# Score tiles placed 64 bytes lower, 64 rows to each score product, and shorter product times in the clocks that order TensorE's work

## The chip, the cores and the metric

The kernel runs on one core of a Trainium2 chip. The metric is the device time of one execution in microseconds, the median of the runs. Engines are named as in the profile: PE is TensorE, DVE is VectorE, ACT is ScalarE, POOL is GpSimd, SP is SyncE (it issues most DMAs here).

## The reference

A layer norm feeds two branches, an attention of 32 heads with 18 columns each and a bilinear feed-forward block; the second, through a SiLU, gates the first.

```python
x = A_x                                   # 1 x 2048 x 576
xn = _layernorm(x, axis=-1)
# _A_ref: H = 32, Dh = 18
scores = jnp.einsum("bhqd,bhkd->bhqk", q, k) * (Dh ** -0.5)
p = _softmax(scores, axis=-1)
o = jnp.einsum("bhqk,bhkd->bhqd", p, v)   # then @ wo
# _B_ref: F = 4608
h = (xn @ w_gate) * (xn @ w_up)           # then h @ w_down
g = _silu(_B_ref(xn, ...))
return x + s * g                          # s: the attention's result
```

All is float32.

## The kernel before

Operands are split into a high and a low part in the fp32r type, and a product of two float32 numbers is made of three: high by high, low by high and high by low. In the scores the three stand below each other in one product: a stack of 3 x 18 = 54 rows, R in the code.

**First stage** (0 to about 193 us): the norm, the turned input (xc, xcx), and the columns of q, k and v. `qk_block(b, c)` makes one block of 128 columns of q and k for one chunk of 512 tokens with 14 products of 128 rows (L493). Its weights are in tiles named wgu, wq or ninth; those of blocks 4 and 5 are in a tile wq2 (wq in the profile) that lies in the pool `early`, at the right end of the memory, with the input and its norm. When the stage is nearly over, the pool `early` is closed and the pool `stk` takes its place with three tiles of 128 x 2048: `turning` and two called `whole`. GpSimd fills them with ones (L638, L641), and `load_stack` (L322) fetches a head's q and k into rows 0 to 53 and 64 to 117.

**The head loop** (about 193 to 2525 us) does the attention and the feed-forward block together. TensorE's array is split in two halves of 64 rows, and the two halves run different products at the same time, r = 0 and r = 1 in the code. The products are:

- `a_item` (L709): 128 queries by 512 keys, 54 rows, for the maximum of each row, which DVE takes (L711). Nearly all on half 0.
- `b_item` (L761): the same scores turned, with two more rows (R + 2 = 56) that hold the negated maximum against ones in the other tile; ACT takes the exponential (L763). Nearly all on half 1.
- `gu_op` (L813): 27 products of 64 rows by 512 columns for each 128 columns of gate (half 1) and of up (half 0).
- `down_op` (L874): products of 64 rows by 288 columns with the weights wd.
- `pv_group` (L772): the exponentials by the values, on all 128 rows with 32 columns. These come in visits, for which both halves are finished first.

Two score products are in `turning` and `whole` at once: one of the two tiles gives the fixed operand, the other the streamed one.

The order of the head loop is worked out when the program is built. `order()` keeps one clock for each half, `clk[0]` and `clk[1]`, and the times at which DVE, ACT and GpSimd come free, and writes down, for the half whose clock is behind, the next product: a score product when it is due and its bank is free by the clocks, otherwise one of the streams `glu` and `down`. Each product moves its half's clock on by a fixed length: 0.231 for a product of 512 columns, 0.132 for one of 288. From the same lengths come the sums `part` and `span`, and with them the pace at which the score products fall due (`pace`, `keep_course`). TensorE then carries out the products strictly in the order written down.

**Last stage** (from about 2525 us): the heads' result by wo (L1469), the gate and the sum.

Of the kernel before, what the change touches and what calls it, by code (L numbers as in the profile page):

```python
# [20 lines left out]
FT = mybir.dt.float32  # L21
# [20 lines left out]
def kernel(  # L42
# [10 lines left out]
    nc = tc.nc  # L53
    _, S, D = x.shape
    F = w_gate.shape[1]
    H = 32
    DH = D // H
    assert S == 2048 and D == 576 and F % 256 == 0
    NT = S // 128
# [40 lines left out]
    ep = early.enter_context(tc.tile_pool(name="early", bufs=1, side="right"))  # L100
# [66 lines left out]
    clk, free, split_at = [0.0, 0.0], {"DVE": 0.0, "ACT": 0.0, "POOL": 0.0}, {}  # L167
# [50 lines left out]
    units = [(c, q) for c in range(NCH) for q in range(NF2)]  # L218
# [90 lines left out]
    R = 3 * DH  # L309
# [257 lines left out]
    def w_now(i):  # L567
        wq[i], todo = w_split(raws[i], 1 if i == 4 else 2, ep if i == 2 else pp if i == 4 else None)
        for f, a in todo:
            f(*a)  # L570
# [36 lines left out]
    for c in range(NCH):  # L607
        if c + 2 < NCH:
            load_x(c + 2)
        for b in range(3):  # L610
            qk_block(b, c)
            if c == 0 and b == 0:
                w_now(2)
        if c + 1 < NCH:
            to_columns(c + 1)
        for b in range(3, 6):
            qk_block(b, c)
            if c == 1 and b == 3:
                v_split(c)
            if b < 5 and c + 2 < NCH:  # L620
                norm(c + 2, (0, 1) if b == 3 else (2, 3))
            if c in (1, 2):
                x_store(c, range(3 * (b - 3), 3 * (b - 2)))
            if c == 0 and b == 3:
                v_fetch(1)
            if c == NCH - 1 and b == 3:
                w_now(3)
        if c == 1:
            w_fetch(3)
            for t in range(4):  # L630
                v_block(t)
            w_fetch(4)
        if c == 2:
            w_now(4)
    early.close()
    stk = ctx.enter_context(tc.tile_pool(name="stk", bufs=1, side="right", reuse_waits="tile"))
    turning = stk.tile([128, S], FR, name="turning")
    nc.gpsimd.memset(turning.bitcast(FT), 1.0)  # L638
    whole = [stk.tile([128, S], FR, name=f"whole{i}") for i in range(2)]
    for w in whole:  # L640
        nc.gpsimd.memset(w.bitcast(FT), 1.0)  # L641
    vmore = ExitStack()
    more_rows(vmore.enter_context(tc.tile_pool(name="vmore", bufs=1, side="right")), 2)
    g_load(0)
# [23 lines left out]
    n = 8  # L668
# [22 lines left out]
    with ExitStack() as mid:  # L691
# [3 lines left out]
        def load_v(g):  # L695
            vt[g] = mp.tile([128, NT, 2 * (DH + 1)], FT, name="vt", bufs=2)
            nc.sync.dma_start(vt[g].rearrange("p t (h d) -> p t h d", h=2), sv[:, 2 * g:2 * g + 2, :].rearrange("(t p) h d -> p t h d", p=128))

        mx = {}

        def a_item(h, i, r=0, tag="a"):

            t, c = divmod(i, 4)
            if i == 0:
                mx[h] = mp.tile([128, NT, 4], FT, name="mx", bufs=1)
            q, k = stacks_of(h, r)
            p = bank(tag, 2)
            rows = slice(64 * r, 64 * r + R)
            nc.tensor.matmul(p, q[rows, t * 128:(t + 1) * 128], k[rows, c * 512:(c + 1) * 512],  # L709
                             start=True, stop=True)  # L710
            nc.vector.tensor_reduce(mx[h][:, t, c:c + 1], p, axis=AX.X, op=OP.max)  # L711
# [42 lines left out]
        def b_item(h, i, r=1, tag="b"):  # L754
            t, c = divmod(i, 4)
            if c % 2 == 0:
                pt[t, c // 2] = mp.tile([128, 2, 512], FT, name="pt", bufs=PT)
            q, k = stacks_of(h, r)
            p = bank(tag, 2)
            rows = slice(64 * r, 64 * r + R + 2)  # L760
            nc.tensor.matmul(p, k[rows, t * 128:(t + 1) * 128], q[rows, c * 512:(c + 1) * 512],  # L761
                             start=True, stop=True)
            nc.scalar.activation(pt[t, c // 2][:, c % 2, :], p, AF.Exp, scale=scale)  # L763
# [37 lines left out]

        hs, us = {}, {}
        TERMS = [t for b in range(9) for t in ((b, b, 0), (9 + b, b, 0), (b, b, 1))]
        half = [slice(0, 64), slice(64, 128)]

        def gu_start(r, n):
            ready(gdone, n)
# [213 lines left out]
            nc.sync.dma_start(wos[1].bitcast(FT), swo[:, 8:10, :])  # L1021

        passed, xdone, xhalf = {}, [], set()

        def stream(r, kind):

            def glu(n):
                c, q = units[n // 2]
                box = []
                for k in range(len(TERMS)):  # L1030
                    def work(k=k):
                        if k == 0:
                            box.append(gu_start(r, n))
                        gu_op(r, n, box[0], k)
                        if q == NF2 - 1 and n % 2 and k % 3 == 2 and c < NCH - 1:
                            b = k // 3
                            if (c, b) in xhalf:
                                x_block(c + 1, b)
                                there["x", c + 1, b] = moved(clk[r] + 0.5, 0.40)
                            xhalf.add((c, b))  # L1040
                        if n == 2 * len(units) - 1 and k == 13:
                            xdone.append(r)
                            if len(xdone) == 2:
                                wo_fetch()
                        if k == len(TERMS) - 1:
                            highs.append((gate_end if r else up_end)(n, box[0]))
                    end = (("DVE", 0.685) if r else ("ACT", 0.595)) if k == len(TERMS) - 1 else None
                    yield 0.231, k == 0, work, end, ("g", n, k), len(TERMS)

            def down(u, n):  # L1050
                own = alone(u, n)
                key = u, n, r * own
                s, i = divmod(n, 2)
                for k in range(len(DTERMS)):
                    def work(k=k):
                        if (own or r == 0) and k == 0:
                            passed[key] = down_start(r, u)
                        down_op(r, u, s, i, passed[key], k, {"POOL": nc.gpsimd, "ACT": nc.scalar, "DVE": nc.vector}[soonest()])
                        if (own or r) and k == len(DTERMS) - 1:
                            acts.append(by_act(u, i, clk[r] + 0.33))  # L1060
                            down_end(u, s, i, passed.pop(key), acts[-1])
                    end = None
                    if (own or r) and k == len(DTERMS) - 1:
                        end = (None, 0.0)
                    yield 0.132, (own or r == 0) and k == 0, work, end, ("d", u, 6 * n + k), len(DTERMS)

            if kind == "g":
                for n in range(2 * len(units)):
                    yield from glu(n)
            else:  # L1070
                for u in range(len(units)):
                    for n in range(8):
                        yield from down(u, n)
# [4 lines left out]
        N = 64  # L1078
        TOTAL = H * N
# [18 lines left out]
        due, jobs, rows_done = [], [], {}  # L1098
        there, queue = {}, [0.0]
        na = nb = 0  # L1100
        part_work = len(units) * (2 * 27 * 0.231 + 4 * 12 * 0.132)
        part = part_work + (TOTAL + N + LEAD) * 0.231
        span = part + H * NT * (0.858 + 0.06)
        QUICK, LAST = 0.65, 0.6
        pace = (PACE * span - QUICK * N - LAST * (N + LEAD)) / (TOTAL - N)
# [3 lines left out]
        def keep_course(now):  # L1109

            left = part_work - (gone[0] + gone[1]) / 2
            left += (2 * TOTAL - na - nb) * 0.1155 + (H * NT - nb // 4 + len(due)) * 0.918
            course[:] = [na, now, (EASE * left - TAIL - LAST * (N + LEAD)) / (TOTAL - na)]

        def a_goal(i):
# [24 lines left out]
        def a_next(r=0):  # L1140
            nonlocal na
            h, i = divmod(na, N)
            stack_turn(0, h, i, 1)
            tag = a_tag()
            a_item(h, i, r, tag)
            slot = turn[tag] % 2
            turn[tag] += 1
            banks[tag][slot] = engine("DVE", clk[r] + 0.43, 0.685) + SPARE
            clk[r] += 0.231
            na += 1  # L1150
            if na % 32 == 0 and N <= na < TOTAL - N:
                keep_course(clk[r])
            if i == N - 1:
                max_fold(h)
                max_split(h, engine("DVE", 0.0, 0.2))
# [5 lines left out]
        def b_next(r=1):  # L1161
            nonlocal nb
            h, i = divmod(nb, N)
            stack_turn(64, h, i, 0)
            if i == 16 and h % 2 == 0 and h // 2 + 1 < H // 2:
                load_v(h // 2 + 1)
            tag = b_tag()
            b_item(h, i, r, tag)
            slot = turn[tag] % 2
            turn[tag] += 1  # L1170
            end = engine("ACT", clk[r] + 0.43, 0.596)
            banks[tag][slot] = end + SPARE
            clk[r] += 0.231
            nb += 1
            if i % 4 == 3:
                due.append((h, i // 4, end + 0.1))
# [343 lines left out]
```

## Time and profile before

| | us |
|---|---|
| median of 3 runs | 2594.28 (2593.94 to 2596.97) |
| span of the profiled execution, first to last instruction | 2590.2 |
| head loop in it | about 193.5 to 2525 |
| products in the head loop | L813 7776, L709 and L761 4096 together, L874 6912 |
| visits of the value products | 67 |

The page gives of the profiled execution its span alone; what lies around it is in the runs' times. A row of groups reads: line, engine, operation, what is written and read, shapes, count, then the busy time, the mean duration of one and the idle time before it. A row of the timeline reads: start and length in us, engine, line, operation, tiles, shape, and the number of equal instructions merged in it. The profile counts a few records of score products under other bank names, so that L709 and L761 show fewer than 2048 each.

### The profile page before, as it was taken

To read this page: it belongs to the slowest core of one execution; us is meant where nothing else is said; L and a number is where in the kernel's file an instruction comes from. 1 tells how busy PE (TensorE), PEld (TensorE's weight loads), DVE (VectorE), ACT (ScalarE), POOL (GpSimd) and SP (SyncE) were. 2 spreads that over 40 slices of the span, in tenths; PEclk is the share of its full clock that TensorE was granted. 3 is DMA by queue.
4 is the path that set the end of the run, shared out by engine and by line. 5 is a ranking of instruction groups with operands and counts; after the bars stand their busy time and mean duration, and the time that the engine had idled before them with its cause. 6 is when DMAs were issued, how large, how long until landed. Compare 5 with 4: busy or idle time off the path is not lost.

```text
span 2590.2 us, 59629 instructions
## 1 busy us (share of the span) xinstructions
PE 2582.3 (100%) x24439; PEld 2124.4 (82%) x24439; DVE 1815.2 (70%) x2996; ACT 1551.5 (60%) x3092; POOL 677.0 (26%) x701
## 2 busy tenths in 40 slices
PE   9999999999999999999999999999999999999999
PEld 8899877888888888888877877778888877877889
DVE  7209777776777778777777877777777777777238
ACT  4224677766766666666666666666666666666621
POOL 3114444434431222222111222111111222221016
PEclk9999999999999999999999999999999999999999
DMA  7899767677653444444454443444444444443357
GB/s 237 258 301 260 200 184 196 184 189 214 178 189 111 141 164 136 150 162 160 143 166 148 142 142 126 137 146 159 121 158 124 145 150 142 133 139 112 125 202 253
DMA packets 186641, 435.65 MB, mean 168 GB/s; under 512 B 51104, under 2 KB 112192, under 8 KB 156160
## 3 DMA queue, kind: packets, MB, share of 16 engines
q1 hardware_dynamic: 184208, 423.88, 53.0%
q0 software_dynamic: 2160, 7.96, 0.8%
q8 instruction: 192, 3.15, 0.5%
q14 instruction: 81, 0.66, 0.1%
HBM read 315.16 MB, written 111.35 MB: 165 GB/s over the span
## 4 chain that ended last, share of the span: by engine, by line
PE 98%; DMA 1%; DVE 1%; SPq 0%; ACT 0%; issue 0%; DVEq 0%
PE pg L813 36%; PE pg L772 17%; PE pg L874 16%; PE pa L709 11%; PE pb L761 9%; PE pb L493 2%; PE pa L493 2%; PE pg L556 2%; PE pg L1469 1%; PE pb L1469 1%; PE pa L1469 1%; DMA oin<-sot 0%; PE pa L761 0%; DMA xin<-in_A_x_dram 0%; PE pg L402 0%; DVE mx L711 0%
## 5 line engine op out<-in xcount | busy, mean ns | idle before, releaser
L711 DVE TENSOR_REDUCE mx<-pa 128x1 f32<-128x512 f32 x2016 | 1349.2, 687 | 330.5 <-PE pa L709 151.5
L813 PE MATMUL pg<-xc,wgu 64*128 64x512 f32 x7776 | 1441.6, 391 | 0.0
L763 ACT ACTIVATE pt<-pb 128x512 f32<-128x512 f32 x2005 | 1145.0, 602 | 469.0 <-PE pb L761 347.3
L813 PEld LDWEIGHTS pg<-xc,wgu 64*128 64x128 f32 x7776 | 1074.9, 186 | 51.9 <-issue 1.0
L874 PE MATMUL pg<-wd,hs 64*128 64x288 f32 x6816 | 879.0, 293 | 0.0
L874 PEld LDWEIGHTS pg<-wd,hs 64*128 64x128 f32 x6816 | 816.3, 185 | 11.3 <-issue 0.8
L709 PE MATMUL pa<-whole,turning 54*128 54x512 f32 x1999 | 783.2, 399 | 0.3 <-DVE mx L711 0.3
L761 PE MATMUL pb<-whole,turning 56*128 56x512 f32 x1978 | 775.2, 398 | 0.0
L772 PE MATMUL pg<-pt,vt 128*32 128x512 f32 x4096 | 453.3, 594 | 0.1
L709 PEld LDWEIGHTS pa<-whole,turning 54*128 54x128 f32 x1999 | 363.3, 184 | 76.6 <-issue 53.0
L854 POOL TENSOR_TENSOR hs<-us,hs 128x512 fp32r<-128x512 f32 x144 | 186.1, 1292 | 865.8 <-ACT hs L838 612.4
L901 POOL TENSOR_TENSOR acc<-acc,st 128x288 f32<-128x288 f32 x284 | 229.5, 810 | 606.3 <-ACT st L931 314.4
L761 PEld LDWEIGHTS pb<-whole,turning 56*128 56x128 f32 x1978 | 360.1, 185 | 5.8
L772 PEld LDWEIGHTS pg<-pt,vt 128*32 128x32 f32 x4096 | 126.2, 110 | 285.1 <-issue 279.2
L778 DVE TENSOR_TENSOR oc<-oc,pg 128x512 f32<-128x512 f32 x35 | 24.1, 688 | 221.1 <-PE pg L772 207.0
L257 POOL TENSOR_TENSOR wgu<-wraw,wgu 128x384 fp32r<-128x384 f32 x108 | 108.2, 1015 | 212.8 <-ACT wgu L256 118.1
L776 ACT ACTIVATE oc<-pg 128x512 f32<-128x512 f32 x32 | 19.2, 599 | 229.4 <-PE pg L772 222.0
L937 DVE TENSOR_TENSOR acc<-acc,pg 128x288 f32<-128x288 f32 x261 | 116.3, 448 | 38.2 <-PE pg L874 35.4
L830 DVE TENSOR_TENSOR us<-pg,us 128x512 f32<-128x512 f32 x144 | 98.7, 685 | 54.9 <-PE pg L813 52.2
L931 ACT ACTIVATE st<-pg 128x288 f32<-128x288 f32 x284 | 117.1, 413 | 27.2 <-PE pg L874 20.0
L823 ACT ACTIVATE us<-pg 128x512 f32<-128x512 f32 x143 | 85.5, 598 | 76.2 <-PE pg L813 63.8
L838 ACT ACTIVATE hs<-us 128x512 fp32r<-128x512 f32 x142 | 89.4, 630 | 16.2 <-DVE us L830 15.8
(164 smaller groups left out, 1294.5 us busy)
## 6 DMA issues: line engine op xcount, KB each, us to landing
wgu<-swg SPq DMA_DIRECT2D x102, 1152.0 KB
wd<-swd SPq DMA_DIRECT2D x50, 1152.0 KB
swg<-wgu SPq DMA_DIRECT2D x36, 1152.0 KB
whole<-sqk SPq DMA_DIRECT2D x192, 144.0 KB
turning<-sqk SPq DMA_DIRECT2D x384, 72.0 KB
swd<-wd SPq DMA_DIRECT2D x18, 1152.0 KB
sqk<-hl SPq DMA_DIRECT2D x32, 512.0 KB
xc<-sx SPq DMA_DIRECT2D x24, 512.0 KB
```

The source lines that it names most:

```text
L257: nc.gpsimd.tensor_tensor(w[:, 9 + b:12 + b, :], raw[:, b:b + 3, :], w[:, b:b + 3, :].bitcast(FT), op=OP.subtract)
L709: nc.tensor.matmul(p, q[rows, t * 128:(t + 1) * 128], k[rows, c * 512:(c + 1) * 512], start=True, stop=True)
L711: nc.vector.tensor_reduce(mx[h][:, t, c:c + 1], p, axis=AX.X, op=OP.max)
L761: nc.tensor.matmul(p, k[rows, t * 128:(t + 1) * 128], q[rows, c * 512:(c + 1) * 512], start=True, stop=True)
L763: nc.scalar.activation(pt[t, c // 2][:, c % 2, :], p, AF.Exp, scale=scale)
L772: nc.tensor.matmul(p[32 * c:32 * c + 32, :], vt[h // 2][:, t, 6 * (h % 2):6 * (h % 2) + 32], pt[t, c // 2][:, c % 2, :], start=t == ts[0], ...
L813: nc.tensor.matmul(ps, gw[n][half[r], a, :], xg[i][half[r], e, :], start=k == 0, stop=k == len(TERMS) - 1)
L854: nc.gpsimd.tensor_tensor(hj[:, 1, :], h32, hj[:, 0, :].bitcast(FT), op=OP.subtract)
L874: op = nc.tensor.matmul(ps[:, 0:HALF], hs[u][half[r], j, a, s * 128:(s + 1) * 128], dw[u][half[r], j, e, i * HALF:(i + 1) * HALF], start=( ...
L901: nc.gpsimd.tensor_tensor(a, a, st, op=OP.add)
L931: nc.scalar.activation(st, ps[:, 0:HALF], AF.Copy)
L937: nc.vector.tensor_tensor(a, a, ps[:, 0:HALF], op=OP.add)
```

## The change

The diff, whole but for unchanged lines:

```diff
@@ first stage, the loop over chunks
             qk_block(b, c)
             if c == 0 and b == 0:
                 w_now(2)
+                ep.tile([128, 16], FT, name="gap")
@@ after early.close()
     turning = stk.tile([128, S], FR, name="turning")
-    nc.gpsimd.memset(turning.bitcast(FT), 1.0)
     whole = [stk.tile([128, S], FR, name=f"whole{i}") for i in range(2)]
-    for w in whole:
-        nc.gpsimd.memset(w.bitcast(FT), 1.0)
+    stk.tile([128, 16], FT, name="gap")
+    for w, low, high in ((turning, 0.0, 1.0), (whole[0], 1.0, 0.0), (whole[1], 1.0, 0.0)):
+        nc.gpsimd.memset(w[32:64].bitcast(FT), low)
+        nc.gpsimd.memset(w[96:128].bitcast(FT), high)
@@ a_item
-            rows = slice(64 * r, 64 * r + R)
+            rows = half[r]
@@ b_item
-            rows = slice(64 * r, 64 * r + R + 2)
+            rows = half[r]
@@ glu, down
-                    yield 0.231, k == 0, work, end, ("g", n, k), len(TERMS)
+                    yield WIDE, k == 0, work, end, ("g", n, k), len(TERMS)
-                    yield 0.132, (own or r == 0) and k == 0, work, end, ("d", u, 6 * n + k), len(DTERMS)
+                    yield SHORT, (own or r == 0) and k == 0, work, end, ("d", u, 6 * n + k), len(DTERMS)
@@ the sums and the clocks
+        WIDE, SHORT = 0.2267, 0.1315
-        part_work = len(units) * (2 * 27 * 0.231 + 4 * 12 * 0.132)
-        part = part_work + (TOTAL + N + LEAD) * 0.231
+        part_work = len(units) * (2 * 27 * WIDE + 4 * 12 * SHORT)
+        part = part_work + (TOTAL + N + LEAD) * WIDE
-            left += (2 * TOTAL - na - nb) * 0.1155 + (H * NT - nb // 4 + len(due)) * 0.918
+            left += (2 * TOTAL - na - nb) * WIDE / 2 + (H * NT - nb // 4 + len(due)) * 0.918
@@ a_next, b_next
-            clk[r] += 0.231
+            clk[r] += WIDE
```

A gap tile takes 64 bytes in each partition at the upper end of its pool, which lies against the right end of the memory, so all other tiles of the pools `early` and `stk` start 64 bytes lower. In bytes from the start of a partition, turning goes from 204768 to 204704, the two whole from 212960 and 221152 to 212896 and 221088, wq2 from 220128 to 220064. All four began 96 above a multiple of 128 and now begin 32 above one. The tiles xc, wgu, hs and wd, which other products read, begin 32 above one before and after.

A score product reads all 64 rows of its half (`half` is rows 0 to 63 and 64 to 127). The added rows are zeros in one tile against ones in the other, so that they add nothing; rows 118 and 119 of half 1 are the rows of the maximum, as before.

Three places in the written order show what moves. The first is GpSimd's order at the point where `stk` is opened, just after the weights' low parts of the first stage. Before:

```order
L133 TENSOR_TENSOR ninth<-wraw,wgu 128x128
L638 MEMSET turning 128x2048
L641 MEMSET whole_1180 128x2048
L641 MEMSET whole_1181 128x2048
L523 MEMSET vo_1187 128x608
```

and with the change:

```order
L642 MEMSET turning 32x2048
L643 MEMSET turning 32x2048
L642 MEMSET whole_1180 32x2048
L643 MEMSET whole_1180 32x2048
L642 MEMSET whole_1181 32x2048
L643 MEMSET whole_1181 32x2048
L523 MEMSET vo_1192 128x608
```

Three memsets of all partitions have become six of 32 partitions with as many columns; what follows them is the same.

The second is TensorE's order just after the 32nd visit of the value products, in the middle of the head loop (at 1281.8 us of the profiled execution). Before:

```order
L772 MATMUL pg<-pt,vt 32x512 x32
L709 MATMUL pa<-whole_1181,turning 128x512
L761 MATMUL pb<-whole_1180,turning 128x512
L709 MATMUL pa<-whole_1181,turning 128x512
L761 MATMUL pb<-whole_1180,turning 128x512
L813 MATMUL pg<-xc,wgu 128x512
L874 MATMUL pg<-wd,hs 128x288
L813 MATMUL pg<-xc,wgu 128x512 x7
L709 MATMUL pa<-whole_1181,turning 128x512
L761 MATMUL pb<-whole_1180,turning 128x512
L813 MATMUL pg<-xc,wgu 128x512 x3
L761 MATMUL pb<-whole_1180,turning 128x512
```

and with the change, after the 32nd visit too:

```order
L775 MATMUL pg<-pt,vt 32x512 x32
L712 MATMUL pa<-whole_1181,turning 128x512
L764 MATMUL pb<-whole_1180,turning 128x512
L712 MATMUL pa<-whole_1181,turning 128x512
L764 MATMUL pb<-whole_1180,turning 128x512
L876 MATMUL pg<-wd,hs 128x288
L815 MATMUL pg<-xc,wgu 128x512
L876 MATMUL pg<-wd,hs 128x288
L815 MATMUL pg<-xc,wgu 128x512
L876 MATMUL pg<-wd,hs 128x288 x2
L815 MATMUL pg<-xc,wgu 128x512
L876 MATMUL pg<-wd,hs 128x288 x2
```

After the same four score products it was mostly gate and up products on both halves that followed, and now short ones are mixed in: the two other streams have moved against the visits. The third place, with the change, is a little after the 36th visit, where gate and up products alone stand between the scores:

```order
L815 MATMUL pg<-xc,wgu 128x512 x4
L712 MATMUL pa<-whole_1181,turning 128x512
L764 MATMUL pb<-whole_1180,turning 128x512
L815 MATMUL pg<-xc,wgu 128x512 x5
L764 MATMUL pb<-whole_1180,turning 128x512
L712 MATMUL pa<-whole_1181,turning 128x512
L815 MATMUL pg<-xc,wgu 128x512 x4
```

There, as before the change, some four wide products stand to one score product of each kind.

The counts of all products, the number of visits (67) and their sizes are the same in both orders.

More of the change, by code (lines that the diff above doesn't have):

```diff
@@ L697, in load_v @@
             nc.sync.dma_start(vt[g].rearrange("p t (h d) -> p t h d", h=2), sv[:, 2 * g:2 * g + 2, :].rearrange("(t p) h d -> p t h d", p=128))
+        half = [slice(0, 64), slice(64, 128)]
         mx = {}
@@ L803 @@
         TERMS = [t for b in range(9) for t in ((b, b, 0), (9 + b, b, 0), (b, b, 1))]
-        half = [slice(0, 64), slice(64, 128)]
         def gu_start(r, n):
@@ L1172, in b_next @@
             banks[tag][slot] = end + SPARE
-            clk[r] += 0.231
+            clk[r] += WIDE
             nb += 1
```

## The prediction

> **What bounds the kernel now.** I read the page first, then TensorE's timeline at four places, then the neighbours it might wait for.
>
> ```profile
> span 2590.2 us, 59629 instructions
> PE 2582.3 (100%) x24439; PEld 2124.4 (82%) x24439; DVE 1815.2 (70%) x2996; ACT 1551.5 (60%) x3092; POOL 677.0 (26%) x701
> PE 98%; DMA 1%; DVE 1%; SPq 0%; ACT 0%; issue 0%; DVEq 0%
> L711 DVE TENSOR_REDUCE mx<-pa 128x1 f32<-128x512 f32 x2016 | 1349.2, 687 | 330.5 <-PE pa L709 151.5
> L813 PE MATMUL pg<-xc,wgu 64*128 64x512 f32 x7776 | 1441.6, 391 | 0.0
> L874 PE MATMUL pg<-wd,hs 64*128 64x288 f32 x6816 | 879.0, 293 | 0.0
> L709 PE MATMUL pa<-whole,turning 54*128 54x512 f32 x1999 | 783.2, 399 | 0.3 <-DVE mx L711 0.3
> L761 PE MATMUL pb<-whole,turning 56*128 56x512 f32 x1978 | 775.2, 398 | 0.0
> L772 PE MATMUL pg<-pt,vt 128*32 128x512 f32 x4096 | 453.3, 594 | 0.1
> ```
>
> TensorE has no idle time, the chain of waits is 98% TensorE, and VectorE waits for TensorE (330.5 us before L711), not the other way. So the time is the sum of TensorE's steps. A matmul row's duration (391 to 399 ns) overlaps its successor's; what counts is the **step**, the time from one start to the next in the same array half. Over the head loop each half does 7776/2 = 3888 gate/up products (L813) and 4096/2 = 2048 score products (L709 and L761, 32 heads of 64 each), all 512 wide, so 5936 wide products, and 6912/2 = 3456 short ones (L874, 288 columns).
>
> The step without scores is read in the tail, where the scores are done:
>
> ```profile
> 2479.62 0.39 PE L813 MATMUL pg<-xc,wgu 64*128 64x512 f32 x1
> ...
> 2480.78 0.39 PE L813 MATMUL pg<-xc,wgu 64*128 64x512 f32 x1
> ...
> 2480.95 11.31 PE L813 MATMUL pg<-xc,wgu 64*128 64x512 f32 x97
> ...
> 2493.09 5.44 PE L874 MATMUL pg<-wd,hs 64*128 64x288 f32 x77
> ...
> 2498.34 0.39 PE L813 MATMUL pg<-xc,wgu 64*128 64x512 f32 x1
> ...
> 2499.48 0.39 PE L813 MATMUL pg<-xc,wgu 64*128 64x512 f32 x1
> ...
> 2499.70 11.28 PE L813 MATMUL pg<-xc,wgu 64*128 64x512 f32 x97
> ```
>
> 97 products over both halves: (11.31 - 0.39)/96 x 2 = 227.5 ns a step, and 226.9 in the last row; I use **227.2**. Short ones: (5.44 - 0.29)/76 x 2 = 135.5 with their hand-overs. With shorts in the other half the gate/up products step 232 ns (2479.62 to 2480.78, five steps) or 226.7 (2498.34 to 2499.70, six).
>
> With scores between them, between two visits of the value products (the stretch after the 32nd visit in the order shown above):
>
> ```profile
> 1283.32 0.39 PE L709 MATMUL pa<-whole,turning 54*128 54x512 f32 x1
> 1283.46 0.39 PE L761 MATMUL pb<-whole,turning 56*128 56x512 f32 x1
> 1283.56 0.63 PE L813 MATMUL pg<-xc,wgu 64*128 64x512 f32 x3
> ...
> 1284.16 0.85 PE L813 MATMUL pg<-xc,wgu 64*128 64x512 f32 x5
> ...
> 1292.51 0.39 PE L709 MATMUL pa<-whole,turning 54*128 54x512 f32 x1
> ```
>
> The two L709 rows are the first and last of 14, 13 periods of (1292.51 - 1283.32)/13 = 0.707 us. A period holds one L709, one L761 and four L813 (rows of 3 and 5 in turn): six wide products on two halves, 2 x 0.707/6 = 235.6 ns. A longer stretch, counted by the grouped view for 1607.1 to 1623.1 us:
>
> ```profile
> L813 PE MATMUL pg<-xc,wgu 64*128 64x512 f32 x97 | 15.8, 392 | 0.0
> L709 PE MATMUL pa<-whole,turning 54*128 54x512 f32 x21 | 8.2, 393 | 0.0
> L761 PE MATMUL pb<-whole,turning 56*128 56x512 f32 x21 | 8.2, 392 | 0.0
> L874 PE MATMUL pg<-wd,hs 64*128 64x288 f32 x2 | 0.4, 292 | 0.0
> ```
>
> 32.0 us of two halves less two shorts, over 139 wide products of which up to four began before the window: 228 to 235. I use **233** where scores run among wide products. Check: 5936 x 0.233 + 3456 x 0.133 (the tail's 135.5 less hand-overs) + 453.3 for L772 = 2296 us, and the loop's row is 2332.5; the other 36 us are edges of 67 visits and waits of one half for the other, which I leave alone.
>
> ```profile
> 193.50:2526.00 2332.50, 2331.37 (x22945) 1897.59 (x22944) 1692.51 (x2762) 1476.35 (x2923) 594.69 (x599) 1.00 0.51 158
> ```
>
> **What makes the scores' neighbourhood slow.** A score product differs from a gate/up product in two things: 54 or 56 rows instead of 64, and the place of its operands. By the allocation, all of xc, wgu, hs and wd begin 32 bytes above a multiple of 128 in each partition; turning and whole begin 96 above, and so does one tile of the first stage, wq2. That stage shows the place alone, with 128 rows throughout:
>
> ```profile
> 37.91 3.19 PE L493 MATMUL pb<-xcx,wq 128*128 128x512 f32 x13
> ...
> 47.53 3.11 PE L493 MATMUL pa<-xcx,wgu 128*128 128x512 f32 x13
> ...
> 59.36 3.19 PE L493 MATMUL pa<-xcx,wq 128*128 128x512 f32 x13
> ...
> 97.91 3.11 PE L493 MATMUL pa<-xc,wgu 128*128 128x512 f32 x13
> ```
>
> Weights from wq2: (3.19 - 0.39)/12 = 233.3 ns; from wgu: (3.11 - 0.39)/12 = 226.7. Same engine, rows and moving tile; only the weights' place differs, and the price, 6.6 ns, is that of the score stretches. So I take the place as the cause and the rows as worth nothing, since 64 rows (227.2) and 128 rows (226.7) step alike.
>
> The Trainium skill (TensorE: Matmul & The Clock Gate, Step-by-step: what each phase is for) says that loading the next weights takes no read bandwidth from the running product, and the Trainium skill (SBUF — State Buffer, Who interferes with whom) that TensorE never waits on anyone for a port. By these the shift buys nothing and the time stays near 2594; the wq rows (233.3 against 226.7) speak against it, so it stands below as a rival with a small chance.
>
> **The change part by part.** After it turning, whole and wq2 begin 32 above like the rest, and a score product has 64 rows: for TensorE it is then a gate/up product that opens and closes its own bank.
> - Wide products with wide ones beside them. Shorts fill 3456 x 0.133 = 460 us of a half, so about 460/1380, a third of the wide ones, have a short beside them; two thirds, 3957, do not. They go from 233 to 227.2: 3957 x 5.8 ns = **23 us**. Bounds: 0, if the wq reading does not carry over, and 5936 x 6.4 = 38 us if all wide ones gain.
> - Wide products with a short beside them, 1979: the tail shows 226.7 and 232 without any score, so most of the excess is the shorts' own. Between 0 and 5.8 ns; I take 1, near the 232 row: **2 us**.
> - Short products: same place, same rows: nothing.
> - wq2: two column blocks of four chunks, 8 x 13 products x 6.6 ns = **0.7 us**.
> - Memsets on GpSimd: three become six of 32 rows. Now:
>
> ```profile
> 108.98 1.81 POOL L638 MEMSET turning<- 128x2048 f32 x1
> 110.83 3.56 POOL L641 MEMSET whole<- 128x2048 f32 x2
> 114.33 1.16 POOL L523 MEMSET vo<- 128x608 f32 x2
> 134.65 1.01 POOL L257 TENSOR_TENSOR wgu<-wraw,wgu 128x384 fp32r<-128x384 f32 x1 [19.15 <-ACT wgu L256]
> 122.32 1.09 SPq L322 DMA_DIRECT2D whole<-sqk x3
> ```
>
>   At the same 1.8 us each (fewer rows, same columns; between 0 and 1.8) they end up to 5.4 us later, vo's at 121; POOL then idled 19.15 us, and SyncE's first load of a stack is issued at 122.3. Covered: 0. With the cover gone, up to 5.4 us.
> - The gap tiles hold nothing. The DMAs and their number stay; scores wait for the same banks.
> - The two clocks draw the order anew, mixing other streams in at other places but with 67 visits and the same products as before, paced at 0.2267 and 0.1315 instead of 0.231 and 0.132. A score period of three wide steps in a half is then 0.68 us instead of 0.707. VectorE must follow:
>
> ```profile
> 1004.64 1.29 DVE L711 TENSOR_REDUCE mx<-pa 128x1 f32<-128x512 f32 x2 [3.86 <-PE pb L761]
> 1282.36 7.74 DVE L711 TENSOR_REDUCE mx<-pa 128x1 f32<-128x512 f32 x11 [5.00 <-PE pb L761]
> ```
>
>   Eleven in 7.74 us is the 0.705 that TensorE feeds it; two in 1.29 us shows 1.29 - 0.687 = 0.60 when two are ready. 0.68 fits, with little over. What the new order gains or loses by itself no row shows; a few us either way, taken as 0.
>
> Sum: 23 + 2 + 0.7 = 25.7 us. The profiled span is 2590.2, and 2594.28, the median, is 4.1 above it; I take that difference as fixed: span 2564.5, time **2569**. After the stretch is shorter VectorE is the next to be late: its share in the loop goes from 1692.5/2332.5, 73%, to 73.4%.
>
> **Rivals.**
> - *Half of it.* Only the score products' own steps shorten, their neighbours' not: 2048 x 5.8 = 12 us, 2582. For: nothing separates own and neighbours' steps cleanly; against: the period of 0.707 is too long for one slow step in three unless that one took 253.
> - *Nothing.* The excess belongs to opening and closing a bank in each score product, or to mixing tiles, and the shift does not touch it: 2594. Against: wq2, whose products share one bank over 14 and still step 233. This is also where the rule of the Trainium skill quoted above leads.
> - *More.* Wide ones beside shorts gain in full too, 5936 x 6.4 = 38 us: 2556.
> - *Slower.* Equal places collide when both halves stream: scores and gate/up products then read in the same lines and each adds the 5.8 ns instead of losing it, 3957 x 5.8 = 23 us on top: 2617. It decides when a score period passes 0.707 us. Against: the tail's two gate/up streams have equal places and step 227.
>
> **How the numbers follow.** Forecast 0.64 (2561 to 2577), half 0.10, nothing 0.11, more 0.08, slower 0.07. Leaving out nothing and slower (0.18), the range runs from 2556 (all wide ones gain) to 2588 (half, with the memsets uncovered). A measurement of this kernel tells about 0.2%, 5 us, from no change: faster 0.64 + 0.10 + 0.08 = 0.82, same 0.11, slower 0.07.
>
> **What would show it.** wq blocks of 13 in 3.11 us instead of 3.19; score stretches without shorts at 227 to 229 ns a step and periods near 0.68 us; score rows nearer 390 than 399 ns; GpSimd's six memsets over before the stacks load; no idle time on TensorE put down to L711. I am wrong if the score stretches still step 232 or more, or if they step 227 while the loop shrinks by much less than 20 us because one half waits for the other or for VectorE.

## The result and the profile after

| | before | after |
|---|---|---|
| median of 4 runs each, us | 2594.11 (2592.69 to 2596.97) | 2568.92 (2568.51 to 2569.37) |
| ratio, 95% interval | | 0.9903 (0.9889 to 0.9917) |
| span of the profiled execution, us | 2590.2 | 2566.7 |
| head loop in it, us | 2332.5 | 2309.6 |

The change makes the kernel 25.2 us faster, 1.0%. The page of the changed kernel, the rows that answer to those shown of before:

```profile
span 2566.7 us, 59619 instructions
PE 2556.5 (100%) x24439; PEld 2109.0 (82%) x24439; DVE 1801.8 (70%) x2995; ACT 1550.5 (60%) x3093; POOL 682.4 (27%) x705
PE 98%; DVE 1%; ACT 0%; DMA 0%; issue 0%; SPq 0%; ACTq 0%; DVEq 0%
L714 DVE TENSOR_REDUCE mx<-pa 128x1 f32<-128x512 f32 x2016 | 1337.3, 686 | 344.9 <-PE pb L764 158.6
L815 PE MATMUL pg<-xc,wgu 64*128 64x512 f32 x7776 | 1370.1, 388 | 0.0
L712 PE MATMUL pa<-whole,turning 64*128 64x512 f32 x1999 | 773.7, 394 | 0.5 <-DVE mx L714 0.3
L764 PE MATMUL pb<-whole,turning 64*128 64x512 f32 x1984 | 769.1, 394 | 0.5 <-ACT pt L766 0.3
```

TensorE still has no idle time and still makes up 98% of the chain, so the gain must lie in its steps. L712 and L764 show half a microsecond of idle time each in the whole span; a wait of one half while the other one runs is not in that figure (e5 below has such a wait). VectorE's idle time has grown from 330.5 to 344.9 us although the span is shorter. The grouped row of the head loop (span, then the busy time of PE, PEld, DVE, ACT and POOL, the granted clock, the DMA share and GB/s):

```profile
193.40:2503.00 2309.60, 2307.61 (x22953) 1883.29 (x22953) 1679.98 (x2764) 1474.40 (x2923) 594.58 (x600) 1.00 0.52 159
```

2332.5 - 2309.6 = 22.9 us of the 23.5 by which the span fell are in the loop, at the same granted clock of 1.00. The timeline of TensorE, first and last of 13 score products of half 0 in a stretch after the 36th visit, where no short product runs:

```profile
1425.84 0.39 PE L712 MATMUL pa<-whole,turning 64*128 64x512 f32 x1
...
1426.52 0.39 PE L712 MATMUL pa<-whole,turning 64*128 64x512 f32 x1
...
1427.43 0.39 PE L712 MATMUL pa<-whole,turning 64*128 64x512 f32 x1
...
1435.36 0.39 PE L712 MATMUL pa<-whole,turning 64*128 64x512 f32 x1
```

Two score products are 3 or 4 steps of their half apart (0.68 or 0.91 us); the twelve intervals alternate, 42 steps in all: (1435.36 - 1425.84)/42 = 226.7 ns, where scores ran at some 235 before. This **ruler** (12 intervals, 42 steps, 36th visit) serves below for every kernel that has the new clocks, and so the same order. It is one stretch of some 9.5 us in one half: it tells whether steps are long, not what that costs over the whole.

TensorE's first stage and GpSimd's memsets:

```profile
35.23 3.11 PE L493 MATMUL pa<-xcx,wq 128*128 128x512 f32 x13
```

```profile
109.13 1.80 POOL L642 MEMSET turning<- 32x2048 f32 x1
...
118.39 1.81 POOL L643 MEMSET whole<- 32x2048 f32 x1
120.25 1.16 POOL L523 MEMSET vo<- 128x608 f32 x2
134.50 1.01 POOL L257 TENSOR_TENSOR wgu<-wraw,wgu 128x384 fp32r<-128x384 f32 x1 [13.09 <-ACT wgu L256]
```

Weights from wq2 now step (3.11 - 0.39)/12 = 226.7 ns. The six memsets take 1.8 us each, as foreseen, and are over at 120.2 us; SyncE issues the first load of a stack at 122.18, and GpSimd still idles 13.09 us behind its memsets.

### The profile page after: what moved, and what is told of

Same layout as the page of the kernel before. It is cut to its first block, busy times and chain, and to the rows that moved or that the text cites. A ratio compares the mean times of both kernels' runs of the same rounds, so it can differ in the third digit from the quotient of the medians.

```text
span 2566.7 us, 59619 instructions
## 1 busy us (share of the span) xinstructions
PE 2556.5 (100%) x24439; PEld 2109.0 (82%) x24439; DVE 1801.8 (70%) x2995; ACT 1550.5 (60%) x3093; POOL 682.4 (27%) x705
## 4 chain that ended last, share of the span: by engine, by line
PE 98%; DVE 1%; ACT 0%; DMA 0%; issue 0%; SPq 0%; ACTq 0%; DVEq 0%
PE pg L815 36%; PE pg L775 18%; PE pg L876 16%; PE pa L712 11%; PE pb L764 8%; PE pb L493 2%; PE pa L493 2%; PE pg L556 2%; PE pg L1472 1%; PE pa L1472 1%; PE pb L1472 1%; DMA xin<-in_A_x_dram 0%; PE pg L402 0%; PE pa L764 0%; DVE mx L714 0%; PE pb L712 0%
## 5 line engine op out<-in xcount | busy, mean ns | idle before, releaser
L714 DVE TENSOR_REDUCE mx<-pa 128x1 f32<-128x512 f32 x2016 | 1337.3, 686 | 344.9 <-PE pb L764 158.6
L815 PE MATMUL pg<-xc,wgu 64*128 64x512 f32 x7776 | 1370.1, 388 | 0.0
L815 PEld LDWEIGHTS pg<-xc,wgu 64*128 64x128 f32 x7776 | 1034.7, 184 | 50.1
L876 PE MATMUL pg<-wd,hs 64*128 64x288 f32 x6816 | 843.2, 293 | 0.0
L876 PEld LDWEIGHTS pg<-wd,hs 64*128 64x128 f32 x6816 | 784.4, 184 | 11.1 <-issue 0.8
L712 PE MATMUL pa<-whole,turning 64*128 64x512 f32 x1999 | 773.7, 394 | 0.5 <-DVE mx L714 0.3
L764 PE MATMUL pb<-whole,turning 64*128 64x512 f32 x1984 | 769.1, 394 | 0.5 <-ACT pt L766 0.3
L712 PEld LDWEIGHTS pa<-whole,turning 64*128 64x128 f32 x1999 | 362.9, 184 | 69.5 <-issue 53.8
L764 PEld LDWEIGHTS pb<-whole,turning 64*128 64x128 f32 x1984 | 360.2, 184 | 6.8 <-ACT pt L766 1.2
```

Source lines behind the costliest of these rows:

```text
L815: nc.tensor.matmul(ps, gw[n][half[r], a, :], xg[i][half[r], e, :], start=k == 0, stop=k == len(TERMS) - 1)
L876: op = nc.tensor.matmul(ps[:, 0:HALF], hs[u][half[r], j, a, s * 128:(s + 1) * 128], dw[u][half[r], j, e, i * HALF:(i + 1) * HALF], start=( ...
```

## The experiments

All times are medians of the runs, all ratios go against the kernel before on the same chip (2593.1, 2593.3 and 2593.7 us in the three sets of runs: e1 to e4, e5 to e8, e9 to e12; 2594.1 beside the changed kernel). Where times of different sets are subtracted below, up to 1 us of the difference can be the set's.

### One part of the change at a time

**e1, the place alone.** The kernel before with the two gap tiles; rows, memsets and clocks as they were.

```diff
@@ first stage
+                ep.tile([128, 16], FT, name="gap")
@@ after whole
+    stk.tile([128, 16], FT, name="gap")
```

> The kernel before with the two gap tiles alone: turning, whole and wq2 begin 32 above a multiple of 128 bytes; 54 and 56 rows to a score product, memsets and both clocks as before, so the order is that of before. Place theory: score stretches without shorts step 227 to 228 ns instead of 233, blocks with wq2 take 3.11 us per 13; 20 to 26 us faster than before, 2568 to 2574. Rows theory: no gain beyond the 0.7 us of wq2, 2593. Clocks theory (the new order brings the gain): 2593 too.

Measured: 2593.24 us, ratio 1.0 (0.999 to 1.0009). Nothing at all, where the prediction had put its 25 us. Its timeline in the first stage, and half 0's score products after the 32nd visit, the stretch and order of the prediction's 0.707:

```profile
35.05 3.11 PE L493 MATMUL pa<-xcx,wq 128*128 128x512 f32 x13
...
1283.78 0.39 PE L711 MATMUL pa<-whole,turning 54*128 54x512 f32 x1
...
1292.90 0.39 PE L711 MATMUL pa<-whole,turning 54*128 54x512 f32 x1
```

and half 1's in the same stretch:

```profile
1283.91 0.39 PE L763 MATMUL pb<-whole,turning 56*128 56x512 f32 x1
...
1290.94 0.39 PE L763 MATMUL pb<-whole,turning 56*128 56x512 f32 x1
```

The wq block has fallen to 3.11, so the tiles did move and the place does count there. But 13 periods of three steps among the scores still take (1292.90 - 1283.78)/39 = 233.8 ns a step, and half 1, whose scores VectorE does not read, takes (1290.94 - 1283.91)/30 = 234.3 (five times 2 and 4 steps). Something else holds them.

**e2, the rows alone.** The changed kernel without the gap tiles and with the old clocks.

```diff
-                ep.tile([128, 16], FT, name="gap")
-    stk.tile([128, 16], FT, name="gap")
-        WIDE, SHORT = 0.2267, 0.1315
+        WIDE, SHORT = 0.231, 0.132
```

> The changed kernel without its gap tiles and with the clocks of before (0.231 and 0.132): 64 rows to each score product and the six memsets, score tiles 96 above a multiple of 128. Place theory: score stretches still step 233 ns, time 2594 plus or minus 3. Rows theory: they step 227 to 228, 2569 to 2574.

Measured: 2590.11 us, 0.9988 (0.9978 to 0.9997): 3 us, barely told from nothing, and 1 us under the range of the place theory. The same stretch:

```profile
1282.02 0.39 PE L710 MATMUL pa<-whole,turning 64*128 64x512 f32 x1
...
1291.20 0.39 PE L710 MATMUL pa<-whole,turning 64*128 64x512 f32 x1
```

(1291.20 - 1282.02)/39 = 235.4 ns a step. In half 0, 64 rows at the old place step as slowly as 54.

**e3, the clocks alone**, and **e4, place and clocks**: the kernel before, and e1, with

```diff
-                    yield 0.231, k == 0, work, end, ("g", n, k), len(TERMS)
+                    yield WIDE, k == 0, work, end, ("g", n, k), len(TERMS)
...
+        WIDE, SHORT = 0.2267, 0.1315
```

and all other lines of the clocks as in the change.

> The kernel before with the clocks 0.2267 and 0.1315 alone: new order, score tiles and rows as before. Place theory: steps stay 233 ns, and the new order by itself is worth at most 5 us either way, 2589 to 2599. Clocks theory: 2569 to 2575.

> The changed kernel with 54 and 56 rows and the memsets of before, so without the rows part. Place theory: 2567 to 2571, the same as the changed kernel. Rows theory: 2590 or more. If rows matter beside a right place, it lies between, 2572 to 2585.

Measured: 2592.52 us, 0.9997 (0.9988 to 1.0006), and 2594.42 us, 1.0004 (0.9995 to 1.0013). The ruler in e3, and then in e4:

```profile
1439.26 0.39 PE L709 MATMUL pa<-whole,turning 54*128 54x512 f32 x1
...
1449.08 0.39 PE L709 MATMUL pa<-whole,turning 54*128 54x512 f32 x1
```

```profile
1439.31 0.39 PE L711 MATMUL pa<-whole,turning 54*128 54x512 f32 x1
...
1449.10 0.39 PE L711 MATMUL pa<-whole,turning 54*128 54x512 f32 x1
```

9.82/42 = 233.8 and 9.79/42 = 233.1 ns: the new order does not shorten a step, and the place does not either as long as the rows are 54 and 56.

**e5, place and rows.** The changed kernel with the old clocks.

```diff
-        WIDE, SHORT = 0.2267, 0.1315
+        WIDE, SHORT = 0.231, 0.132
```

> The changed kernel with the clocks of before: place and 64 rows together, order of before's lengths. The place alone and the rows alone left the steps beside scores at 232 to 233 ns. Theory of two disturbers, each enough by itself: with both gone the steps fall to 228 and the time to 2569 to 2575. Theory that all three edits are needed: above 2588.

Measured: 2575.60 us, 0.9929 (0.9914 to 0.9944), 0.6 us above the range of the two disturbers. So the parts do not add up: place 0, rows 3, together 17.7 (2593.3 - 2575.6); and the clocks, worth 0.6 by themselves, are worth 6.7 on top of the two (2575.60 - 2568.92). In the stretch after the 32nd visit the two halves differ; half 0 (12 periods) and half 1 (two of three steps hold a gate product, so 6 intervals of 2 and 4 steps, 18 steps):

```profile
1274.45 0.39 PE L712 MATMUL pa<-whole,turning 64*128 64x512 f32 x1
1274.56 0.39 PE L764 MATMUL pb<-whole,turning 64*128 64x512 f32 x1
...
1275.84 0.39 PE L712 MATMUL pa<-whole,turning 64*128 64x512 f32 x1
...
1278.64 0.39 PE L764 MATMUL pb<-whole,turning 64*128 64x512 f32 x1
...
1282.79 0.39 PE L712 MATMUL pa<-whole,turning 64*128 64x512 f32 x1
```

Half 1 steps 4.08/18 = 226.7 ns, half 0 8.34/36 = 231.7. They have equal rows and places; what the trace shows of half 0 is a wait for banks. `a_item` has two banks and uses them in turn. The first score above, of 1274.45, is read by VectorE, and the weights of the next but one, which writes the same bank, are loaded after that:

```profile
1274.88 0.69 DVE L714 TENSOR_REDUCE mx<-pa 128x1 f32<-128x512 f32 x1
```

```profile
1275.62 0.18 PEld L712 LDWEIGHTS pa<-whole,turning 64*128 64x128 f32 x1
```

The reduce ends at 1275.57, the load follows 0.05 us later, and its product starts at 1275.84, 1.39 us after the first. With two banks that is a score every 0.695 us, which is the period measured (8.34/12), while three steps of 226.7 ns would be 0.680. It does not show as idle time, since half 1 runs on. In the changed kernel's ruler two intervals have seven steps, 1.587 us, and the banks are free in time.

The banks need not be all of it. In e2, with the same order, half 0 is the slower one too (235.4 ns against 6.94/30 = 231.3 for half 1, L762 from 1282.15 to 1289.09), and there the weights of its scores are loaded as soon as the product before them has started. And how much of the 6.7 us the banks are remains open: e12 below has such stretches too (L712 at 1427.61, 1428.30, 1428.99, 1429.68 and 1430.37, 0.69 us apart) and is the fastest of all.

### Sixty-four rows, or equal rows?

e1 to e5 allow two readings: 64 rows and the place 32 are good in themselves, or score products must be **like their neighbours**. The next four kernels part them.

**e7, all products with 56 rows.** Scores, gate, up and down alike, the place as in the change.

```diff
-        half = [slice(0, 64), slice(64, 128)]
+        half = [slice(0, 56), slice(64, 120)]
```

> The changed kernel with 56 rows in every product of the halves, scores, gate/up and down alike; 8 of 64 rows of the gate/up and down sums are left out, so its result is another. Theory of sameness (a step is longer where neighbours differ in rows): all products alike again, steps 227 to 228, 2567 to 2573. Theory of full groups (rows that do not fill groups of 32 are slow): steps 232 or more everywhere, also in the tail without scores, 2588 or more.

Measured: 2568.14 us, 0.9901 (0.9886 to 0.9916). The ruler:

```profile
1425.10 0.39 PE L712 MATMUL pa<-whole,turning 56*128 56x512 f32 x1
...
1434.62 0.39 PE L712 MATMUL pa<-whole,turning 56*128 56x512 f32 x1
```

9.52/42 = 226.7 ns, to the nanosecond that of 64 rows. The number of rows costs nothing; a difference in it does.

**e8, 56 rows in b_item alone**, 64 in a_item.

```diff
@@ b_item
-            rows = half[r]
+            rows = slice(64 * r, 64 * r + R + 2)
```

> The changed kernel with 56 rows in b_item's products alone, a_item's at 64. If each odd product costs its own share: half of the rows' loss, about 2579 to 2583. If one odd product in the neighbourhood is enough: 2586 or more. If only 54 rows were bad: 2569 to 2573.

Measured: 2588.65 us, 0.9982 (0.9973 to 0.9991): 56 rows in one of the two kinds of score products give back 20 of the 25 us. In its timeline half 1 (L764) is to be read against half 0 (L712), which had 64 rows throughout:

```profile
1438.78 0.39 PE L764 MATMUL pb<-whole,turning 56*128 56x512 f32 x1
1438.86 0.39 PE L712 MATMUL pa<-whole,turning 64*128 64x512 f32 x1
...
1442.97 0.39 PE L764 MATMUL pb<-whole,turning 56*128 56x512 f32 x1
...
1445.21 0.39 PE L712 MATMUL pa<-whole,turning 64*128 64x512 f32 x1
```

Half 1: 6 intervals of three steps, 4.19/18 = 232.8 ns. Half 0: 8 intervals, 28 steps, 6.35/28 = 226.8. What counts is what runs in the same half.

**e11, everything 64 bytes higher.** No gap tile in `early` and `stk`, but one below all that stood at 32, so that all tiles begin 96 above a multiple of 128.

```diff
@@ consts, below xc, wgu, hs and wd
+    consts.tile([128, 16], FT, name="gap")
@@ early, stk
-                ep.tile([128, 16], FT, name="gap")
-    stk.tile([128, 16], FT, name="gap")
```

> The changed kernel without its two gap tiles, and with one gap tile of 64 bytes among the constants instead, so that all other tiles move up: xc, wgu, hs, wd, turning, whole and wq2 all begin 96 above a multiple of 128. Theory of sameness (a step is longer where neighbours differ in place): 2567 to 2572, wq2's blocks take 3.11 us per 13. Theory that 32 is a good place and 96 a bad one: 2590 or more, and long steps in the tail without scores too.

Measured: 2568.86 us, 0.9905 (0.9888 to 0.9921), the time of the changed kernel. The ruler:

```profile
1425.13 0.39 PE L711 MATMUL pa<-whole,turning 64*128 64x512 f32 x1
...
1434.65 0.39 PE L711 MATMUL pa<-whole,turning 64*128 64x512 f32 x1
```

226.7 ns at 96, and wq2's 13 products take 3.11 us. The place before the change was not bad; it was another than the neighbours'.

**e10, the score tiles 128 bytes lower still.** By a multiple of 128 they stand where xc, wgu, hs and wd do; by a multiple of 256 they do not (32 against 160).

```diff
-    stk.tile([128, 16], FT, name="gap")
+    stk.tile([128, 48], FT, name="gap")
```

> The changed kernel with turning and whole another 128 bytes lower: still 32 above a multiple of 128, but 32 above a multiple of 256 where xc, wgu, hs and wd are 160 above one. If places count modulo 128 or less: 2567 to 2571. If modulo 256 or more: 2586 or more.

Measured: 2587.13 us, 0.9975 (0.9965 to 0.9984). The ruler:

```profile
1434.81 0.39 PE L712 MATMUL pa<-whole,turning 64*128 64x512 f32 x1
...
1435.51 0.40 PE L712 MATMUL pa<-whole,turning 64*128 64x512 f32 x1
...
1436.44 0.39 PE L712 MATMUL pa<-whole,turning 64*128 64x512 f32 x1
...
1437.14 0.40 PE L712 MATMUL pa<-whole,turning 64*128 64x512 f32 x1
...
1438.08 0.39 PE L712 MATMUL pa<-whole,turning 64*128 64x512 f32 x1
...
1438.77 0.40 PE L712 MATMUL pa<-whole,turning 64*128 64x512 f32 x1
...
1439.71 0.39 PE L712 MATMUL pa<-whole,turning 64*128 64x512 f32 x1
...
1440.41 0.40 PE L712 MATMUL pa<-whole,turning 64*128 64x512 f32 x1
...
1441.34 0.39 PE L712 MATMUL pa<-whole,turning 64*128 64x512 f32 x1
...
1442.04 0.40 PE L712 MATMUL pa<-whole,turning 64*128 64x512 f32 x1
...
1442.98 0.39 PE L712 MATMUL pa<-whole,turning 64*128 64x512 f32 x1
...
1443.67 0.40 PE L712 MATMUL pa<-whole,turning 64*128 64x512 f32 x1
...
1444.61 0.39 PE L712 MATMUL pa<-whole,turning 64*128 64x512 f32 x1
```

9.80/42 = 233.3 ns. All rows are shown because they also tell whose steps lengthen. The six intervals of three steps (0.70, 0.70, 0.69, 0.70, 0.70, 0.69) make 4.18/18 = 232.2 ns a step, the six of four 5.62/24 = 234.2. Were the excess that of the score product alone, one in each interval, the longer intervals would have the smaller mean, 226.7 + 5.5 x 3/4 = 230.8. So the gate and up products between the scores are slow too.

128 bytes, with the same instructions in the same order, cost 18.2 us (2587.13 - 2568.92). So places that agree by a multiple of 128 bytes are not enough. A multiple of 256 is: in the changed kernel turning begins at 204704 and xc, by the allocation, at 59552, which is 567 x 256 bytes away and no multiple of 512, and the step is 226.7.

### Which of the two operands?

**e6, the streamed one off** (`whole` 64 bytes higher, at 96), and **e9, the fixed one off** (`turning` at 96).

```diff
@@ e6
+    stk.tile([128, 16], FT, name="gap")
     whole = [stk.tile([128, S], FR, name=f"whole{i}") for i in range(2)]
-    stk.tile([128, 16], FT, name="gap")
```

```diff
@@ e9
+    stk.tile([128, 16], FT, name="gap")
     whole = [stk.tile([128, S], FR, name=f"whole{i}") for i in range(2)]
-    stk.tile([128, 16], FT, name="gap")
+    stk.tile([128, 16], FT, name="gap2")
```

> The changed kernel with the gap between turning and the two whole: turning (the fixed operand of nearly all score products) 32 above a multiple of 128, whole (the streamed operand) 96 above. If the streamed operand's place disturbs: steps beside scores 232 to 233, 2588 to 2594. If only the fixed operand's does, as the weights of wq2 did: 228, 2569 to 2573.

> The changed kernel with turning (the fixed operand) 96 above a multiple of 128 and whole (the streamed one) 32 above, by gaps of 64 bytes before and after the two whole. With the streamed operand alone off, the time was 2588.7. If either operand off is enough: 2586 or more, steps beside scores 231 to 233. If only the streamed one matters: 2569 to 2573.

Measured: e6 2588.69 us, 0.998 (0.997 to 0.999); e9 2580.64 us, 0.9951 (0.9936 to 0.9966). The ruler in e6, and then in e9:

```profile
1436.55 0.39 PE L712 MATMUL pa<-whole,turning 64*128 64x512 f32 x1
...
1446.27 0.39 PE L712 MATMUL pa<-whole,turning 64*128 64x512 f32 x1
```

```profile
1431.80 0.39 PE L713 MATMUL pa<-whole,turning 64*128 64x512 f32 x1
...
1441.50 0.39 PE L713 MATMUL pa<-whole,turning 64*128 64x512 f32 x1
```

9.72/42 = 231.4 and 9.70/42 = 231.0 ns. Either operand alone does it, and the streamed one costs more over the whole (19.8 against 11.7 us above the changed kernel), though the ruler hardly tells them apart; e9 has the steps expected if either is enough, but a time between the two ranges. The two do not add either: both off by 128 (e10) cost 18.2, less than the streamed one off by 64.

Two cases tell what must agree with what. In e10 the two operands of a score product agree with each other and differ from the neighbours', and the steps are long. In the first stage before the change 13 products in a row were all alike, with weights from wq2 at 96 and xcx streamed from 32 (by the allocation), and stepped 233.3. So like neighbours are not enough either: the fixed and the streamed operands of all of them have to stand at one place.

### The clocks by what was measured

**e12, clocks nearer to the steps of the changed kernel.** In the changed kernel's trace the mean step, taken from the starts of successive products of a half between two visits, is about 228.4 ns for wide products and 132.5 for short ones; both were set.

```diff
-        WIDE, SHORT = 0.2267, 0.1315
+        WIDE, SHORT = 0.2284, 0.1325
```

> The changed kernel with the clocks at the mean steps measured in it, 0.2284 and 0.1325, instead of 0.2267 and 0.1315. If the order gains by clocks that equal the chip's steps: 2563 to 2568. If the worth of an order is chance within a few us: 2564 to 2576 without relation to it. If clocks must not be longer than the step of an undisturbed product, 0.2267: 2571 to 2576, as with 0.231.

Measured: 2567.32 us (2567.23 to 2567.99), 0.9899 (0.9884 to 0.9914). It is the fastest of all, 1.6 us under the changed kernel and 1.5 under e11, which has the changed kernel's order and ran in the same set (2568.19 to 2569.04). The runs do not overlap, but the intervals of the ratios do, so this gain is likely, not settled. The time lies in the first range expected and in the second, so it does not tell an order that gains by matching clocks from chance.

## Why the prediction was right, and where it was not

The time came out as predicted, 2568.92 against 2569, but by luck: two errors of some 7 us cancelled.

- **What bounds the kernel** held: the time is the sum of TensorE's steps. 22.9 of the 23.5 us in the span are in the loop, at steps of 226.7 ns where no short products run, and TensorE is still 98% of the chain.
- **The failed step** is "So I take the place as the cause and the rows as worth nothing, since 64 rows (227.2) and 128 rows (226.7) step alike". The two rows come from stretches in which all products were alike, and those show only that a number of rows costs nothing in itself (e7 confirms it for 56). They could not show what a *difference* in rows among neighbours costs. By that step e1 had to give the gain, and gave none. In its place the runs show a condition of two parts: where no short products run and no bank is late, a half steps 226.7 ns if the products that follow each other agree in rows and all their operands in places, and 231 to 236 if either differs. Before the change both differed, so taking away one left the other to cost nearly all of it.
- **"What the new order gains or loses by itself no row shows; a few us either way, taken as 0"** was off by 6.7 us. By itself it is 0.6 (e3), as taken; on top of the equal steps it is 6.7 (e5 against the changed kernel). Why the order gains is open: the waits for banks seen in e5 are part of it at most, and that the planner's lengths match the steps was not shown apart from where the streams happen to fall.
- **"0.68 fits, with little over"** failed for VectorE. It was worked out from two reduces in 1.29 us, when two are ready; it left out that a bank comes free only after product, reduce and the next load, 1.39 us for two scores. In the old order with equal rows and places (e5) that is the period of half 0, 0.695. The new order gets by because every second period in the ruler has four steps.
- **The sum**: 25.7 us for place and rows together were 17.7 (e5); 25.7 - 17.7 = 8 too much there, 6.7 too little for the clocks. The term of 3957 x 5.8 ns assumed every wide product without a short beside it to reach 227.2; in e5's stretch half 0 stayed at 231.7, no faster than its banks' turn. The 4.1 us "taken as fixed" between span and median were 2.2 after the change (2568.92 - 2566.7), and the span came out at 2566.7, not 2564.5.
- **A reading**: 235.6 ns for the stretch after the 32nd visit is half 0's. Half 1's L761 in it, from 1283.46 to 1290.43, step 6.97/30 = 232.3; the 233 used lies between.
- **wq2** (3.11 us a block) and the **memsets** (covered, at 1.8 us each) came as worked out.
- **Rivals.** *Nothing* had a reason that fell, and a time that e1 showed to be right for the place alone. The rule behind it is the Trainium skill's (SBUF — State Buffer, Who interferes with whom: TensorE waits for no one at a port). What the prediction drew from it, that the shift buys nothing, does not hold: e10 changes nothing but 128 bytes of address, and the steps among scores go from 226.7 to 233.3 ns. Whether that is a wait at a port, no run shows. *Half*, that only the scores' own steps are long, fell with the rows of e10, and in the kernel before the three steps of half 0 from 1283.32 on are 233, 236 and 236 ns, the gate and up products' too. *Slower* fell with the ruler: equal places do not collide. *More* had nothing for it, 13 us below the time.
- **The checks named** came in, 3.11, 226.7 and 0.68 (for every second period); score rows at 394 ns lie midway between the 390 and 399 named. All of them would have been met had the place been the whole cause: they tested that the steps shortened, not why. Only a kernel with one part of the change could tell.

## What to carry to other kernels

Where TensorE runs without a gap, give products that follow each other in one half the same number of rows (zeros fill them up) and let all their operands, fixed and streamed, agree in place by a multiple of 256 bytes, both at once: here 0.7%, and 0 or 3 us for half of it. Then look whether the next limit, here a bank's turn of 1.39 us, still fits the shorter steps. A reading taken where everything is alike prices no difference, so before a cause is credited with a gain, ask whether another property differs in the same places. Setting the planner's lengths anew was worth 6.7 us here after the steps had changed, and 0.6 before.

## What the runs showed of the hardware

- A product of 512 columns with a load of new weights before it steps 226.7 ns in its half, whether of 56, 64 (e7, after) or 128 rows (the first stage), and whether its operands begin at 32 or at 96 above a multiple of 128 bytes (after, e11).
- Rows that differ within the half: 232.8 to 234.3 ns (e8, e4, e1). Places that differ by 64 bytes: 231.0 or 231.4 with one operand, 235.4 with both in half 0 (e9, e6, e2), 233.3 with the weights alone in the first stage (before); by 128 bytes: 233.3 (e10). Places 567 x 256 bytes apart: 226.7 (after). The two do not add: with both, 233.8 in the new order (e3) and 235.6 in the old (the prediction's stretch).
- A bank whose score VectorE reads is written again 1.39 us after the score before it began (e5): product to reduce 0.43, reduce 0.69, 0.05 to the next load, 0.22 from there to its product.
- It is open by what mechanism the steps lengthen, how the 6.7 us of the new order come about, and why half 0 is slower than half 1 in e2. It was not tried to give the down products whose weights begin 128 bytes off by their place in wd (slices of 1152 bytes) the place of the rest.
